# A fused backward pass on one Trainium2 core: output stores on GpSimd's queue, a last buffer of its own, and row sums scheduled earlier

## The chip, the core and the metric

The kernel runs on one core of one Trainium2 chip (trn2). A core has TensorE (PE, with its weight loads shown apart as PEld), VectorE (DVE), ScalarE (ACT), GpSimd (POOL) and SyncE (SP). All of them read their instructions in order from their own queue, and DMA transfers are issued from such a queue too. The metric is the device time of one execution in microseconds; the median of several runs is compared.

## The reference

The forward function is `x + A(xn, k, v) + B(xn)` on 2048 rows of 512 columns in bf16, and what is to be computed is its value and its gradients with respect to nine inputs.

```python
xn = _layernorm(x, axis=-1)
# A: k_shift = sum of four shifted copies of k, each times a column of shift_k
#    kv = k_shift * v
#    y  = causal convolution of kv with ssm_k along the sequence (by FFT) + kv * ssm_D
#    A  = xn * y
# B: h = (xn @ w_gate) * (xn @ w_up);  B = h @ w_down
return x + _A_ref(xn, ...) + _B_ref(xn, ...)
...
_out, _vjp = jax.vjp(_f, A_q, A_k, A_v, A_shift_k, A_ssm_k, A_ssm_D, B_w_gate, B_w_up, B_w_down)
return (_out, *_vjp(grad_out))
```

The outputs that matter here: out_0 is the value, out_1 the gradient of x, out_2 of k, out_3 of v (each 2048 x 512), out_4 of shift_k, out_5 of ssm_k, out_6 of ssm_D, out_7 and out_8 of w_gate and w_up (512 x 1376), out_9 of w_down (1376 x 512).

## The kernel before

The 2048 rows lie as 128 partitions of R = 16 rows, so a tile such as `yC` is [128, 16, 512]. The first 300 us or so (`main`, lines 858 to 876, with `side` woven into it) compute the gated network by chunks of rows, its input gradients (left in DRAM as `BX`), and the convolutions through transforms whose results are left in DRAM as `GD`. The hidden activations are left in DRAM as `HDD`.

The change is in the last stage (lines 902 to 1183). Its backbone is the generator `dw` (L1030): for each of the 11 blocks of 128 hidden columns (the last has 96) it computes the gradient of w_down (`down_grad`, L1008, matmuls L1012, cast to `od`), turns the hidden activations (`hid_t`, L832, matmuls L845, from tiles `hb` loaded from `HDD` at L791; the last three blocks come turned by a transposing DMA, `natT`, L806), and computes the gradients of w_gate and w_up (matmuls L1048 into `pu`). ACT casts `pu` into `og` (L1055), a tile with one buffer that holds two blocks, and SP stores it (L1059) after every second block and after the last one.

Four side generators are woven in by hand. `dw` yields 6 times a block, and the loop at L1176 takes one step of a side at its start index n and then every 2 or 3 yields (L1175):

- `inv_y` (L930), start 0, step 3: the inverse transform (matmuls L918 from tiles `g`, loaded at L783 two buffers deep) of y into `yC` and of the gradient `dd`, four rows at a time; DVE multiplies `dd` by v into `dks` (L948) and by the stored k-shift into `kb` (L949), which SP stores to out_3 (L950). The tiles `vb` and `kb` are loaded two buffers deep (L923, L925). Lines 953 and 954 copy three rows of `dks` across partitions. `load_kh` (L1143) loads `khC`, a copy of k with its halo rows.
- `dsk_gram` (L1065), start 27: the gradient of shift_k, matmuls L1071 from `dks` and `khC`.
- `inv_dk` (L975), start 35: the gradient of ssm_k, into `o5t`, which takes over the memory of `khC` (tag `o5k`) and is stored at L994.
- `ew` (L1162), start 10: first a load of `bb` (L1111, from `BX`), then sixteen pieces of VectorE work: `final(b)` (L1114), the value `o` and the gradient of x, `e`, for two rows of each partition, and `bwd(b)` (L1093), the gradient of k, `dk`. Each ends with a store on SP: L1124, L1139, L1105. The tiles `o0` and `e` have one buffer, `dk`, `bb`, `vb`, `kb` and `dd` have two.

Within this frame a planner of the framework orders the instructions of each engine by its own model of when they are ready; `tc.high_priority` moves DVE's products ahead, and `tc.issue_after(ins)` keeps DMA issues behind a given one on the same queue. A queue is strictly in order: an issue that waits (for the engine that makes its data, or for a buffer) holds all behind it. Except for one store of `BX` and half of the last `od`, SP issues every DMA of this stage.

Of the kernel before, what the change touches and what calls it, by code (L numbers as in the profile page):

```python
# [8 lines left out]
BF = mybir.dt.bfloat16  # L9
# [9 lines left out]
D = 512  # L19
F = 1376  # L20
R = 16
P = 128
NC4 = 4
# [167 lines left out]
def kernel(  # L191
# [24 lines left out]
    nc = tc.nc  # L216
# [409 lines left out]
    def seq(*its):  # L626
        for it in its:
            for _ in it:
                yield
# [291 lines left out]
    def load_vk(r0):  # L921
        vb = c2b.tile([P, 2, D], BF, name="vb")
        nc.sync.dma_start(vb[:], v_n[:, r0:r0 + 2, :])  # L923
        kb = c2b.tile([P, 2, D], BF, name="kb")
        DKS["kb", r0] = nc.sync.dma_start(kb[:], KS[:, r0:r0 + 2, :])  # L925
        return vb, kb
# [2 lines left out]

    def inv_y():  # L930
        gq = pend
        todo = [(sg, r0) for r0 in range(0, R, 4) for sg in (0, 1)][2:]
        for r4 in range(0, R, 4):
            gy = gq.pop(0)
            vk = [load_vk(r4), load_vk(r4 + 2)]
            for i in range(0, 4, 2):
                st1p(gy, i, yC[:, r4 + i:r4 + i + 2, :])
            if todo:
                gq.append(load_g1(*todo.pop(0)))
            yield  # L940
            gd = gq.pop(0)
            for i in range(0, 4, 2):
                r0 = r4 + i
                vb, kb = vk.pop(0)
                dd = c2b.tile([P, 2, D], BF, name="dd")
                st1p(gd, i, dd[:])
                with tc.high_priority(offset=SOON):
                    nc.vector.tensor_tensor(dks[:, r0:r0 + 2, :], dd[:], vb[:], op=ALU.mult)  # L948
                    nc.vector.tensor_tensor(kb[:], dd[:], kb[:], op=ALU.mult)  # L949
                DKS[r0] = nc.sync.dma_start(o3_n[:, r0:r0 + 2, :], kb[:])  # L950
                if r0 == 2:
                    nc.gpsimd.memset(dks[96:128, R:R + 3, :], 0.0)
                    nc.sync.dma_start(dks[0:112, R:R + 3, :], dks[1:113, 0:3, :])
                    nc.sync.dma_start(dks[112:127, R:R + 3, :], dks[113:128, 0:3, :])
            if todo:
                gq.append(load_g1(*todo.pop(0)))
            if r4 == R - 8:
                load_kh()
            yield

    def load_gk(rq):
# [13 lines left out]
    def inv_dk():  # L975
        o5t = c2.tile([P, NC4, P, R], BF, name="o5t", tag="o5k")
        o5 = out_5.rearrange("(c q) s -> c q s", q=P)
        for rq in range(4):
            gk = gks.pop(0)
            if rq == 0:  # L980
                gk_last = load_gk_last()
            for b in range(2):
                po = P2("po", [P, 2, 4, P])
                for h in range(2):
                    for i in range(4):
                        for c in range(2):
                            nc.tensor.matmul(po[:, h, i, :], lhsT=(gk_last(c, i) if rq == 3 else gk[:, c, i])[:, cs(2 * b + h)], rhs=TB.IW[:, c, :],
                                             start=(c == 0), stop=(c == 1))
                act(o5t[:, 2 * b:2 * b + 2, :, 4 * rq:4 * rq + 4], po[:].rearrange("q h r s -> q h s r"))
                if b == 1 and rq < 2:  # L990
                    gks.append(load_gk(2) if rq == 0 else None)
                if rq == 3:
                    for c in (2 * b, 2 * b + 1):
                        nc.sync.dma_start(o5[c], o5t[:, c].rearrange("q s r -> q (s r)"))  # L994
                yield
            if rq == 0:
                yield from put_dD(o5t)
# [32 lines left out]
    def dw():  # L1030
        og = None
        load_hb(2)
        for fb, (f0, fw) in enumerate(FBLK):
            last = fb + 1 == NFB
            if not last:
                down_grad(fb)
                yield
                hid_t(fb + 1, 0)
                hid_t(fb + 1, 1)
                yield  # L1040
                yield
            pu = P2("pu", [P, NC4, 2, P])
            if fb % 2 == 0:
                og = c2.tile([P, 2, NC4, 2 * P], BF, name="og")
            q0 = (fb % 2) * P
            for c in range(NC4):
                for r in range(R):
                    nc.tensor.matmul(pu[:, c, :, :fw], lhsT=xnC[:, r, cs(c)], rhs=nat_d(fb, r),  # L1048
                                     start=(r == 0), stop=(r == R - 1))
                if c == 1:  # L1050
                    yield
                    if fb + 1 in TURNED:
                        last_t(fb + 1)
                    yield
            act(og[:, :, :, q0:q0 + fw].rearrange("p t c f -> p c t f"), pu[:, :, :, :fw])  # L1055
            if fb % 2 == 1 or last:
                a = f0 - q0
                for t, o in enumerate((out_7, out_8)):
                    nc.sync.dma_start(o[:, a:f0 + fw].rearrange("(c p) f -> p c f", p=128), og[:, t, :, :q0 + fw])  # L1059
            yield  # L1060
            if last:
                down_grad(fb)
                yield
# [29 lines left out]
    def bwd(b):  # L1093
        rb = slice(2 * b, 2 * b + 2)
        dk = c2b.tile([P, 2, D], BF, name="dk")
        t = c2.tile([P, 2, D], BF, name="tk", tag="dxn")
        for j in range(4):
            src = dks[:, 2 * b + j:2 * b + j + 2, :]
            w = skb[:, j:j + 1, :].to_broadcast((P, 2, D))
            if j == 0:  # L1100
                nc.vector.tensor_tensor(dk[:], src, w, op=ALU.mult)
            else:
                nc.vector.tensor_tensor(t[:], src, w, op=ALU.mult)  # L1103
                nc.vector.tensor_tensor(dk[:], dk[:], t[:], op=ALU.add)  # L1104
        nc.sync.dma_start(o2_n[:, rb, :], dk[:])  # L1105

    FL = {}

# [5 lines left out]
    def final(b):  # L1114
        if b + 1 < 8:
            load_fin(b + 1)
        bb = FL.pop(b)
        rb = slice(2 * b, 2 * b + 2)
        tt = nc.vector.tensor_tensor
        stt = nc.vector.scalar_tensor_tensor  # L1120
        o = c2.tile([P, 2, D], BF, name="o0")
        tt(o[:], xnC[:, rb], yC[:, rb], op=ALU.mult)
        tt(o[:], o[:], bb[:, :, 0, :], op=ALU.add)
        nc.sync.dma_start(o0_n[:, rb, :], o[:])  # L1124
        e = c2.tile([P, 2, D], BF, name="e")
        tt(e[:], goC[:, rb], yC[:, rb], op=ALU.mult)
        dxn = c2.tile([P, 2, D], F32, name="dxn")
        for i in range(2):
            r = 2 * b + i
            stt(dxn[:, i], e[:, i], 1.0, bb[:, i, 1, :], op0=ALU.mult, op1=ALU.add, accum_out=s1[:, r:r + 1])  # L1130
            stt(e[:, i], dxn[:, i], 1.0, xnC[:, r, :], op0=ALU.mult, op1=ALU.mult, accum_out=s2[:, r:r + 1])  # L1131
        nc.vector.tensor_scalar(m2[:, rb], s2[:, rb], -1.0 / D, None, op0=ALU.mult)
        stt(m1[:, rb], s1[:, rb], -1.0 / D, rstd[:, rb], op0=ALU.mult, op1=ALU.mult)
        for i in range(2):
            r = 2 * b + i
            stt(dxn[:, i], xnC[:, r, :], m2[:, r:r + 1], dxn[:, i], op0=ALU.mult, op1=ALU.add)  # L1136
            nc.vector.tensor_scalar(e[:, i], dxn[:, i], rstd[:, r:r + 1], m1[:, r:r + 1], op0=ALU.mult, op1=ALU.add)
        tt(e[:], e[:], goC[:, rb], op=ALU.add)
        nc.sync.dma_start(o1_n[:, rb, :], e[:])  # L1139

    KH = []

    def load_kh():  # L1143
        khC = c2.tile([P, R + 3, D], BF, name="khC", tag="o5k")
        nc.gpsimd.memset(khC[0:1, 0:3, :], 0.0)
        with tc.issue_after(LG["g"].ins):
            nc.sync.dma_start(khC[:, 3:3 + R, :], k_n)
            nc.sync.dma_start(khC[1:113, 0:3, :], k_n[0:112, R - 3:R, :])
            nc.sync.dma_start(khC[113:128, 0:3, :], k_n[112:127, R - 3:R, :])
        KH.append(khC)  # L1150

    def every(gen, start, step):
        return [start, step, gen]
# [6 lines left out]
    tail.append(lambda: bwd(7))  # L1160

    def ew():  # L1162
        with tc.issue_after(DKS[2].ins):
            load_fin(0)
        yield
        for f in tail:
            f()
            yield

    def load_dk():  # L1170
        gks.append(load_gk(0))
        gks.append(load_gk(1))
        yield

    sides = [every(seq(inv_y(), load_dk()), 0, 3), every(dsk_gram(), 27, 2), every(inv_dk(), 35, 3), every(ew(), 10, 3)]  # L1175
    for n, _ in enumerate(dw()):  # L1176
        for sd in sides:
            if n >= sd[0]:
# [35 lines left out]
```

## Time and profile before

| | us |
|---|---|
| median of 3 runs | 489.93 (489.39 to 490.7) |
| the profiled execution | 486.87 |
| its span, first to last instruction | 485.0 |
| PE busy | 470.9 (97%) |
| DVE busy | 342.1 (71%) |
| ACT busy | 316.9 (65%) |
| POOL busy | 15.3 (3%), none of it DMA issues |
| granted TensorE clock, mean | 0.995 |
| DMA, mean over the span | 288 GB/s |

The profile is one execution. The durations quoted below come from it, so a sum is made against 486.87 and its span, not against the median. A row of the timeline reads: start, length, engine, line, operation, output <- inputs, count, and in brackets how long the engine had been idle and what ended that. "SPq" rows are DMA issues on SP's queue: their length is the time on the queue and not that of the transfer. In the list of waits a row reads: who waited for whom, total us, times, longest.

From 300 to 478 us the stage described above runs. DVE's busy share in it is uneven: 8.88 us busy of the 52.8 from 300 to 352.8, 105.94 of the 119 from 352.8 to 471.8. The DMA engines are busy for 0.94 of 319 to 351, 0.97 of 351 to 390 and 0.64 of 442 to 478.

### The profile page before, as it was taken

Reading aid. Unit: us, or ns where it says so; the run is one execution under the profiler, and the core shown is the slowest. Engines: PE = TensorE matmul, PEld = TensorE weight load, DVE = VectorE, ACT = ScalarE, POOL = GpSimd, SP = SyncE. Lnnn points to the kernel's source line nnn. Section 1 sums busy time; section 2 is a strip of 40 time slices with the busy share of each in tenths; the row PEclk is TensorE's granted clock in tenths of the full one; section 3 lists DMA queues with packets and bytes.
Section 4 is the critical chain, followed back from the end, with each engine's and each line's share of the span. In section 5 each row is a group of like instructions: output and inputs, shape, how many; then the busy total and the mean of one; then the engine's idle time right before and its main releaser. Section 6 shows DMA issues by size and latency. Waiting matters only on the chain.

```text
span 485.0 us, 10518 instructions
## 1 busy us (share of the span) xinstructions
PE 470.9 (97%) x4335; PEld 314.3 (65%) x4335; DVE 342.1 (71%) x623; ACT 316.9 (65%) x353; POOL 15.3 (3%) x31
## 2 busy tenths in 40 slices
PE   7998999999999999999999999999999999999994
PEld 7866754547647448447457744567777788777792
DVE  7889979988265667686777875013277899998880
ACT  4976896759568678779779955476567624643330
POOL 8010000000000000000000000020000000000000
PEclk9999999999999999999999999999999999999998
DMA  8999999999997968868977289998999989599717
GB/s 271 375 380 354 295 264 325 339 310 341 306 311 228 279 196 267 261 222 241 297 239 253 88 320 321 389 336 295 338 390 371 369 275 398 195 286 263 230 53 266
DMA packets 105775, 139.88 MB, mean 288 GB/s; under 512 B 33372, under 2 KB 78849, under 8 KB 104063
## 3 DMA queue, kind: packets, MB, share of 16 engines
q1 hardware_dynamic: 104142, 137.84, 85.9%
q10 hardware_dynamic: 1584, 1.36, 1.0%
q8 instruction: 34, 0.56, 0.5%
q14 instruction: 15, 0.11, 0.1%
HBM read 68.45 MB, written 63.41 MB: 272 GB/s over the span
## 4 chain that ended last, share of the span: by engine, by line
PE 57%; DVE 24%; DMA 14%; issue 2%; ACT 2%; SPq 1%; ACTq 0%; DVEq 0%
PE px L553 15%; PE pgu L510 13%; PE py L546 8%; PE pdh L516 6%; DMA out_dram<-o 5%; PE pf L368 3%; PE ps L582 3%; PE pg L611 3%; DVE tk L1103 2%; DVE dk L1104 2%; PE pu L1048 2%; DMA HDD<-hd 2%; DVE dxn L1136 2%; DVE dxn L1130 2%; DVE e L1131 2%
## 5 line engine op out<-in xcount | busy, mean ns | idle before, releaser
L553 PE MATMUL px<-WT,hd 128*128 128x512 bf16 (+1 forms) x352 | 81.1, 380 | 0.0
L1048 PEld LDWEIGHTS <-xnC 128*128 128x128 bf16 x704 | 67.1, 98 | 8.8 <-issue 0.9
L553 PEld LDWEIGHTS <-hd 128*128 128x128 bf16 (+1 forms) x352 | 32.8, 98 | 44.4 <-issue 7.7
L1048 PE MATMUL pu<-natd,xnC 128*128 128x256 bf16 x512 | 58.5, 273 | 0.2 <-ACT nath L235 0.2
L235 ACT CAST GO<-pg 128x1024 bf16<-128x1024 f32 x48 | 46.2, 1015 | 13.8 <-issue 7.2
L235 ACT CAST SP<-ps 128x1024 bf16<-128x1024 f32 x47 | 45.6, 1026 | 13.8 <-PE ps L582 11.9
L235 ACT CAST gu<-pgu 128x1024 bf16<-128x1024 f32 (+1 forms) x48 | 45.4, 945 | 13.6 <-PE pgu L510 13.5
L598 DVE TENSOR_TENSOR T<-SP 128x2048 bf16<-128x2048 bf16 x24 | 29.4, 1223 | 34.8 <-ACT SP L235 34.7
L510 PE MATMUL pgu<-xt,Wu 128*128 128x256 bf16 (+1 forms) x352 | 53.1, 274 | 0.6 <-DVE fst L238 0.4
L510 PE MATMUL pgu<-xt,Wg 128*128 128x256 bf16 (+1 forms) x352 | 52.8, 273 | 0.3 <-DMA Wg<-in_B_w_gate_dram 0.3
L516 PE MATMUL pdh<-gt,WdT 128*128 128x256 bf16 (+1 forms) x352 | 47.1, 273 | 0.1
L235 ACT CAST og<-pu 128x1024 bf16<-128x1024 f32 (+1 forms) x11 | 10.9, 993 | 50.0 <-PE pu L1048 25.6
L510 PEld LDWEIGHTS <-Wu 128*128 128x128 bf16 (+1 forms) x352 | 33.0, 100 | 14.5 <-issue 9.8
L546 PE MATMUL py<-Wd,hd 128*128 128x512 bf16 (+1 forms) x176 | 41.4, 380 | 0.0
L235 ACT CAST fst<-pf 128x1024 bf16<-128x1024 f32 x40 | 39.0, 1032 | 0.8 <-ACT dh L235 0.5
L235 ACT COPY natd<-pt 128x2048 bf16<-128x2048 bf16 x16 | 30.0, 1874 | 13.4 <-PE pt L845 13.4
L516 PEld LDWEIGHTS <-WdT 128*128 128x128 bf16 (+1 forms) x352 | 34.9, 100 | 5.2 <-issue 0.2
L510 PEld LDWEIGHTS <-Wg 128*128 128x128 bf16 (+1 forms) x352 | 34.8, 100 | 4.2 <-DMA Wg<-in_B_w_gate_dram 0.6
L530 DVE TENSOR_TENSOR hd<-gu 128x512 bf16<-128x512 bf16 (+1 forms) x48 | 19.1, 398 | 17.5 <-ACT gu L235 17.5
L531 DVE TENSOR_TENSOR hd<-gu,dh 128x1024 bf16<-128x1024 bf16 (+1 forms) x48 | 30.8, 643 | 0.8
L1012 PE MATMUL pd<-goC,nath 128*128 128x512 bf16 x128 | 30.1, 379 | 0.0
L546 PEld LDWEIGHTS <-hd 128*128 128x128 bf16 (+1 forms) x176 | 16.4, 98 | 20.5 <-issue 3.1
(176 smaller groups left out, 703.3 us busy)
## 6 DMA issues: line engine op xcount, KB each, us to landing
HDD<-hd SPq DMA_DIRECT2D x35, 384.0 KB, 3.9
FD<-fst SPq DMA_DIRECT2D x24, 512.0 KB, 4.4
X<-FD SPq DMA_DIRECT2D x24, 512.0 KB, 5.0
GD<-GO SPq DMA_DIRECT2D x24, 512.0 KB, 3.8
g<-GD SPq DMA_DIRECT2D x11, 1024.0 KB, 9.2
hb<-HDD SPq DMA_DIRECT2D x8, 1344.0 KB, 9.0
bb<-BX SPq DMA_DIRECT2D x8, 512.0 KB, 8.2
BX<-bx SPq DMA_DIRECT2D x7, 512.0 KB, 4.0
```

The source lines that it names most:

```text
L235: nc.scalar.copy(o, i)
L368: nc.tensor.matmul(pf[:, c, :], lhsT=TB.W1[:, c, :], rhs=src[:, i, :], start=True, stop=not point)
L510: nc.tensor.matmul(pgu[:w, i, t, :], lhsT=W[:, c, f0:f0 + w], rhs=xt[:, :, c, :], start=(c == 0), stop=(c == NC4 - 1))
L516: nc.tensor.matmul(pdh[:w, i, :], lhsT=WdT[:, c, f0:f0 + w], rhs=gt[:, :, c, :], start=(c == 0), stop=(c == NC4 - 1))
L530: nc.vector.tensor_tensor(hd[:fw, fb0:fb0 + n, 0, :], gu[:fw, :n, 0, :], gu[:fw, :n, 1, :], op=ALU.mult)
L531: nc.vector.tensor_tensor(hd[:fw, fb0:fb0 + n, 1:3, :], gu[:fw, :n], dh[:fw, :n].unsqueeze(2).to_broadcast((fw, n, 2, 256)), op=ALU.mult)
L546: nc.tensor.matmul(py[:], lhsT=hd[:fw, fb, 0, ss], rhs=Wd[:fw, fb, :], start=(fb == 0), stop=(fb == NFB - 1))
L553: nc.tensor.matmul(px[:], lhsT=hd[:fw, fb, t, ss], rhs=W[:fw, fb, :], start=(t == 1 and fb == 0), stop=(t == 2 and fb == NFB - 1))
L582: nc.tensor.matmul(ps[32 * q:32 * q + 32, a, :], lhsT=TB.EF[64 * a:64 * a + 64, 4 * g + q, ri].rearrange("p k j -> p (k j)"), rhs=X[64 * a ...
L598: tt(W[:].rearrange("p c a d -> p c (a d)"), A[:, i:i + 1].rearrange("p c a d -> p c (a d)").to_broadcast((P, 2, 2 * D)), B[:].rearrange(" ...
L1012: nc.tensor.matmul(pd[:fw, :], lhsT=nat_h(fb, r), rhs=goC[:, r, :], start=(r == 0), stop=(r == R - 1))
L1048: nc.tensor.matmul(pu[:, c, :, :fw], lhsT=xnC[:, r, cs(c)], rhs=nat_d(fb, r), start=(r == 0), stop=(r == R - 1))
```

## The change

It touches only the last stage:

- the stores of `o`, `e`, `dk` and `kb`, and the two copies between partitions of `dks`, are issued from GpSimd's queue instead of SP's;
- `e` gets two buffers;
- the `ew` side (the sums of `final` and `bwd`) starts at step 4 instead of 10, and its first `bb` load goes behind the latest `g` load instead of behind a `kb` store;
- the last `og` gets a tile of its own, `og1`, in a buffer of the tag `dd` (same size, [128, 2, 4, 128] bf16);
- `khC` is allocated and its first rows cleared at the start of `inv_y`; it is loaded one round later, behind the last `kb` load instead of behind the last `g` load.

```diff
     def inv_y():
         gq = pend
+        khC = c2.tile([P, R + 3, D], BF, name="khC", tag="o5k")
+        nc.gpsimd.memset(khC[0:1, 0:3, :], 0.0)
+        KH.append(khC)
...
             vk = [load_vk(r4), load_vk(r4 + 2)]
+            if r4 == R - 4:
+                load_kh()
...
-                DKS[r0] = nc.sync.dma_start(o3_n[:, r0:r0 + 2, :], kb[:])
+                nc.gpsimd.dma_start(o3_n[:, r0:r0 + 2, :], kb[:])
                 if r0 == 2:
                     nc.gpsimd.memset(dks[96:128, R:R + 3, :], 0.0)
-                    nc.sync.dma_start(dks[0:112, R:R + 3, :], dks[1:113, 0:3, :])
-                    nc.sync.dma_start(dks[112:127, R:R + 3, :], dks[113:128, 0:3, :])
+                    nc.gpsimd.dma_start(dks[0:112, R:R + 3, :], dks[1:113, 0:3, :])
+                    nc.gpsimd.dma_start(dks[112:127, R:R + 3, :], dks[113:128, 0:3, :])
             if todo:
                 gq.append(load_g1(*todo.pop(0)))
-            if r4 == R - 8:
-                load_kh()
             yield
...
             if fb % 2 == 0:
-                og = c2.tile([P, 2, NC4, 2 * P], BF, name="og")
+                og = c2b.tile([P, 2, NC4, P], BF, name="og1", tag="dd") if last else c2.tile([P, 2, NC4, 2 * P], BF, name="og")
...
-        nc.sync.dma_start(o2_n[:, rb, :], dk[:])
+        nc.gpsimd.dma_start(o2_n[:, rb, :], dk[:])
...
-        nc.sync.dma_start(o0_n[:, rb, :], o[:])
-        e = c2.tile([P, 2, D], BF, name="e")
+        nc.gpsimd.dma_start(o0_n[:, rb, :], o[:])
+        e = c2.tile([P, 2, D], BF, name="e", bufs=2)
...
-        nc.sync.dma_start(o1_n[:, rb, :], e[:])
+        nc.gpsimd.dma_start(o1_n[:, rb, :], e[:])
...
     def load_kh():
-        khC = c2.tile([P, R + 3, D], BF, name="khC", tag="o5k")
-        nc.gpsimd.memset(khC[0:1, 0:3, :], 0.0)
-        with tc.issue_after(LG["g"].ins):
+        khC = KH[0]
+        with tc.issue_after(DKS["kb", R - 2].ins):
             nc.sync.dma_start(khC[:, 3:3 + R, :], k_n)
             nc.sync.dma_start(khC[1:113, 0:3, :], k_n[0:112, R - 3:R, :])
             nc.sync.dma_start(khC[113:128, 0:3, :], k_n[112:127, R - 3:R, :])
-        KH.append(khC)
...
     def ew():
-        with tc.issue_after(DKS[2].ins):
+        with tc.issue_after(LG["g"].ins):
             load_fin(0)
...
-    sides = [every(seq(inv_y(), load_dk()), 0, 3), every(dsk_gram(), 27, 2), every(inv_dk(), 35, 3), every(ew(), 10, 3)]
+    sides = [every(seq(inv_y(), load_dk()), 0, 3), every(dsk_gram(), 27, 2), every(inv_dk(), 35, 3), every(ew(), 4, 3)]
```

## The prediction

> **What bounds the kernel now.** I read the busy time by stage first, then the timeline of the last twelve microseconds, then the waits of SP's queue, and last how long the loads take to land. The stage that the diff touches starts at about 300 us. This row of the windows view has the busy us of PE, PEld, DVE, ACT and POOL, then the granted clock, the DMA share and GB/s:
>
> ```profile
> 300.00:478.00 178.00, 177.71 (x1665) 133.04 (x1662) 114.82 (x233) 85.68 (x75) 2.74 (x2) 1.00 0.88 300
> ```
>
> PE is busy for 177.71 of 178 us at full clock. So no edit to VectorE's work, SP's queue or the stores can shorten this stretch; they can only open holes in it. DVE has 63 us of idle time. The chain of waits runs through DVE from 344 us on, which only says who released whom last. What a change can win lies after PE's last matmul. The timeline of the end:
>
> ```profile
> 474.15 0.33 PE L1048 MATMUL pu<-nat,xnC 128*128 128x192 bf16 x2
> ...
> 477.33 0.59 PE L1012 MATMUL pd<-goC,nat 128*96 128x512 bf16 x2
> ...
> 480.16 0.80 ACT L235 CAST og<-pu 128x768 bf16<-128x768 f32 x1 [9.89 <-DMA out_dram<-og]
> 480.86 0.37 ACT L235 CAST od<-pd 96x256 bf16<-96x256 f32 x1
> ...
> 481.26 0.42 DVE L238 CAST od<-pd 96x256 bf16<-96x256 f32 x1 [9.55 <-ACT od L235]
> 482.01 0.47 SPq L1025 DMA_DIRECT2D out_dram<-od  x1
> ```
>
> PE ends at 477.33 + 0.59 = 477.92. The last `og` cast could have run at 474.48, when its matmuls ended, but waited until 480.16: `og` has one buffer, and the store of its previous contents had not landed. The two casts of the last `od` stand behind it on ACT. Why that store was late shows in SP's queue:
>
> ```profile
> 467.38 4.69 SPq L1105 DMA_DIRECT2D out_dram<-dk  x2
> 472.17 0.68 SPq L1020 DMA_DIRECT2D out_dram<-od  x1
> 472.94 0.96 SPq L994 DMA_DIRECT2D out_dram<-o5t  x2
> 473.99 2.22 SPq L1059 DMA_DIRECT2D out_dram<-og  x2
> ```
>
> The previous `og` was cast by 469.35 (ACT, 468.34 + 1.01), but SP stood at the last `dk` store until DVE had made it (471.71), then issued an `od` and two `o5t` that had been ready since 461 to 462, and reached `og` at 473.99. The second half of that store landed 4.99 us after 475.08, at 480.07. So the end is a store that waited for DVE in SP's queue, and then a buffer that waited for the store.
>
> **The parts, and what each costs.**
>
> 1. *Own last buffer.* `og1` takes a slot of `dd`, whose last reader (L949) ended at 390.4. The last `og` cast then starts 0.04 us after its matmuls (the offset that ACT's `od` cast shows at 447.64 behind PE's 447.60), so at 474.52, and ends at 475.32. ACT is free when PE ends, and the first `od` cast starts at 477.92 + 0.04 = 477.96 instead of 480.86. What follows it (second cast, SP's issue 0.47, 2.0 us to landing, the end of the span at 485.0) took 4.14 us and stays. Term: 477.96 - 480.86 = **-2.90 us**. Next late is PE itself.
>
> 2. *Stores of o, e, dk, kb by GpSimd* (32 stores and the two copies of `dks`). They leave SP, whose queue from 319 to 485 waited for DVE like this (us in total, times, longest):
>
> ```profile
> SPq L1139 <- DVE e L1138: 25.5, 5, 6.5
> SPq L1105 <- DVE dk L1104: 13.6, 4, 3.9
> SPq L950 <- DVE kb L949: 10.4, 7, 4.6
> ```
>
> At the end this alone would free the `og` store: issue at 469.4, and with 4.99 us landed at about 475, so it is nearly a second remedy for the same 2.90 us and adds nothing to part 1. Elsewhere SP issues `hb`, `g`, `vb`, `bb` earlier; PE hardly waited for them, so that is worth 0.2 us at most and I take 0. On POOL the stores wait in the order in which DVE makes them, so none waits behind a later product. Behind them stands only the memset L952, whose rows bwd(7) alone needs.
>
> The cost of a store issued by POOL is in no row. Below: SP's own 0.34 us, so no loss. Above: POOL's memsets, 1.37 us each, 34 x 1.37 = 47 us of a POOL that was busy 2.74 us in the stretch. Only one of these stores is waited for by something on PE's path: `kb`, whose two buffers are refilled by SP. Call L the time from DVE's product to the landing. SP's `kb` stores landed in 2.0 to 7.0 us; with POOL's upper 1.37 that is 8.4, my value, since the memset is POOL's only row here. The upper end is the longest landing of any 256 KB store, 10.7 us, plus two issues in a row, 2.7: 13.4.
>
> What L must meet: SP puts the load of `kb` 10 ahead of the `g` load for rows 12 to 15. kb 6 is made by DVE at 346.6, `g` takes 9.5 us to land and is used by PE at 368.08, so with 0.5 for issue 346.6 + L + 10.0 <= 368.08, or L <= 11.5. The load one block earlier gives 330.0 + L + 9.7 <= 351.5, L <= 11.8. At 8.4 there is no stall; at 13.4 a stall of 1.9 us.
>
> [...]
>
> 3. *Final sums six places sooner.* In the schedule by hand, the first `bb` load moves from SP 347.01 (behind the `kb` stores) to behind the `g` load at about 327.3. With the 5.9 to 10.6 us that `bb` took to land, DVE can begin near 336 instead of 352.90. Its work from 352.8 to 471.8 is 105.94 us busy in 119, plus 2.5 us of dks/kb products that now fall inside: 336 + 108.4 = 444.4. That moves DVE's end away from the end of the kernel by 27 us; off PE's path, worth 0.
>
> 4. *e in two buffers.* SP's hold of L1126 goes; DVE only. Worth 0.
>
> 5. *khC loaded behind the last kb load* instead of behind the `g` load (364.65). kb 14 needs the buffer of kb 10, made at 363.1: 363.1 + 8.4 = 371.5, then 0.5 for issue and 13.3 to land gives 385.3. PE first reads khC at 390.09: 4.8 us spare, so 0. It turns late at L = 13.2. In exchange `hb` 5, whose load went out at 374.98 because SP stood at `e`, can go at about 366.6.
>
> **Sum.** Span 485.0 - 2.9 = 482.1; with the 1.87 us around it (486.87 - 485.0) 484.0 for the profiled execution. The median of the runs, 489.93, lies 3.06 us above that execution, and I carry the difference over: 489.93 - 2.90 = **487.0 us**. What this kernel's measurement can tell from no change is about 0.3%, 1.5 us.
>
> **Rivals.**
>
> *A: stores hold up the loads (slower).* The `kb` buffer comes free late, SP stands at the `kb` load (L925), and the `g` load behind it comes late. It decides at L = 11.5. For: in-order SP, saturated DMA (next rival), GpSimd stores of unknown length. Against: POOL has nothing else to do, and DVE is only 2.5 us busy between 335 and 352.8. Price: at L = 17, 5.5 us at `g`; khC's 3.8 us lies inside that shift. 487.0 + 5.5 = 492.5. At 13.4 it is 488.9, still counted as faster by a little.
>
> *B: the same bytes sooner, into a full DMA.* From 340 to 380 the DMA share reads 1.00 and 1.02 at 361 to 364 GB/s. Starting 17 us sooner puts about five `bb` loads, four o, four e and three dk before 380, where there were three, two, two and none: 1.0 + 0.5 + 0.5 + 0.75 = 2.75 MB more, or 7.6 us at 361 GB/s. The `g` loads have about 3.5 us spare (issue 338.9 to use 351.5, less 9.2), so up to 4 us of stall: 491.1; with the spare rate of 319 to 351 (322 GB/s) half of it: about 489. Against: `hb` and the stores had up to 20 us spare, and the peaks of the 40 slices reach 416 GB/s.
>
> *C: the end is set by something else, no change.* If the last stores queue at the DMA as before (full from 472 to 480), freeing ACT does nothing: 489.9. Against: 1 MB of `o5t` can leave at 462, and what is left after 469.4 (0.5 + 1.0 + 0.2 MB) takes 4.6 us at 370 GB/s.
>
> *D: GpSimd's descriptors hold up DVE.* DVE has 477.9 - 444.4 = 33.5 us spare over 34 stores, so it decides at 1.0 us of blocking a store. At 1.37 DVE ends at 491 and the time is about 499. Against, in the timeline: the memset on POOL at 320.44 runs beside DVE's L1122 and L1126, and these take 0.69 us as everywhere else.
>
> ```profile
> 320.44 1.37 POOL L952 MEMSET dks<- 32x1536 bf16 x1 [292.79 <-ACT yC L235]
> ...
> 320.46 0.69 DVE L1122 TENSOR_TENSOR o<-xnC,yC 128x1024 bf16<-128x1024 bf16 x1 [12.11 <-ACT yC L235]
> ...
> 321.07 0.69 DVE L1126 TENSOR_TENSOR e<-goC,yC 128x1024 bf16<-128x1024 bf16 x1
> ```
>
> **How the numbers follow.** The forecast, 487.0, holds with 0.57. A has 0.15: 0.05 short of 488.4 (faster), 0.02 within the bound, 0.08 slower. B has 0.15: 0.02 faster, 0.09 same, 0.04 slower. C has 0.08, same. D has 0.05, slower. So faster 0.64, same 0.19, slower 0.17. The low end is the forecast less the spread of the runs shown (0.65 us): 486.3; PE's end forbids more. The high end takes in B's 491.1 and leaves A's long stores and D out: 491.1.
>
> **What would show it.** Right: PE's busy share stays at 1 up to an end near 478; ACT casts `og1` within 0.1 us of its matmuls; the first `od` cast follows PE's end by 0.04 us; the span ends 4.1 us after it; DVE ends before 455; SP has no wait for L1104, L1138 or L949. Wrong: a wait of PE for `g`, `hb`, khC or `pq` between 340 and 395 (A if SP stands at L925 before it, B if the load was issued in time and landed late), a last POOL store after 480, DVE durations above 0.69 us while POOL issues (D).

## The result and the profile after

The change makes the kernel slower: 515.69 us against 490.31 for the kernel before (medians of six runs each), a ratio of 1.0515 (95% interval 1.0473 to 1.0557). The forecast was 487.0 with 491.1 as its upper end. The profiled execution took 516.29, its span is 514.6 us, 29.6 more than the 485.0 of before. Line numbers of the changed kernel are 3 to 5 higher than in the kernel before (the `dks` product is L953 there and L948 here; the `kd` product L1080 and L1077).

The windows row of the same 178 us in the changed kernel (PE, PEld, DVE, ACT, POOL busy, clock, DMA share, GB/s):

```profile
300.00:478.00 178.00, 153.69 (x1362) 110.54 (x1361) 113.28 (x233) 79.11 (x66) 21.66 (x36) 0.94 0.84 285
```

PE had 177.71 us of this window before and has 153.69 now. The list of PE's waits in the changed kernel (who waited for whom, total, times, longest) names the holes:

```profile
PE pt L845 <- DVE kd L1080: 12.2, 2, 11.0
PE pq L918 <- DMA g<-GD: 5.1, 1, 5.1
PE pk L1074 <- DMA khC<-in_A_k_dram: 4.7, 1, 4.7
...
PE pk L1074 <- DVE dks L953: 1.4, 2, 0.8
```

Before, none of these four rows exists. They sum to 23.4 us, with 0.5 more for `dskt`. PE's own work takes longer too: in the stage it is busy for 184.47 us (from 302.1 on) instead of 177.41 (from 300.3 on) with the same 1663 records, 7.1 us more, since it runs at a lower granted clock behind the long holes (0.74 from 420 to 440). And the tail, from PE's last matmul to the end of the span, went from 485.0 - 477.92 = 7.1 to 514.6 - 510.88 = 3.7 us. 23.9 + 7.1 - 3.4 = 27.6 of the 27.8 by which the stage grew. The other 1.8 of the 29.6 lie ahead of it: the same product (`bx`, L548) starts at 302.32 instead of 300.53, in code that the change does not touch.

**The tail did what was forecast.** The timeline of the changed kernel's end:

```profile
507.47 0.80 ACT L235 CAST og<-pu 128x768 bf16<-128x768 f32 x1 [4.25 <-PE pu L1051]
...
510.29 0.59 PE L1015 MATMUL pd<-goC,nat 128*96 128x512 bf16 x2
510.96 0.37 ACT L235 CAST od<-pd 96x256 bf16<-96x256 f32 x1 [2.70 <-PE pd L1015]
...
511.81 0.34 SPq L1028 DMA_DIRECT2D out_dram<-od  x1
```

The last `og` cast waits for its own matmuls and no longer for a store; the first `od` cast follows PE by 0.08 us (510.96 against 510.88). So the 3.4 us are won, at the end of a PE that is 33 us late.

**The holes come through VectorE.** First, how it worked before, between two rounds of `inv_y` (timeline of DVE, kernel before):

```profile
344.09 0.69 DVE L948 TENSOR_TENSOR dks<-dd,vb 128x1024 bf16<-128x1024 bf16 x1 [12.91 <-ACT dd L235]
344.70 0.69 DVE L949 TENSOR_TENSOR kb<-dd,kb 128x1024 bf16<-128x1024 bf16 x1
...
352.90 0.69 DVE L1123 TENSOR_TENSOR o<-o,bb 128x1024 bf16<-128x1024 bf16 x1 [6.32 <-DMA bb<-BX]
...
360.66 0.69 DVE L948 TENSOR_TENSOR dks<-dd,vb 128x1024 bf16<-128x1024 bf16 x1 [1.32 <-ACT dd L235]
```

DVE waits for `dd`, makes the `dks` and `kb` products, and only then stands for something of the sums (`bb`). Now the same two rounds in the changed kernel:

```profile
346.79 0.69 DVE L1141 TENSOR_TENSOR e<-e,goC 128x1024 bf16<-128x1024 bf16 x1
354.36 0.69 DVE L1129 TENSOR_TENSOR e<-goC,yC 128x1024 bf16<-128x1024 bf16 x1 [6.88 <-ACT od L235]
354.96 0.69 DVE L953 TENSOR_TENSOR dks<-dd,vb 128x1024 bf16<-128x1024 bf16 x1
355.56 0.69 DVE L954 TENSOR_TENSOR kb<-dd,kb 128x1024 bf16<-128x1024 bf16 x1
...
371.66 0.69 DVE L1129 TENSOR_TENSOR e<-goC,yC 128x1024 bf16<-128x1024 bf16 x1 [4.13 <-DMA out_dram<-e]
...
378.31 0.68 DVE L953 TENSOR_TENSOR dks<-dd,vb 128x1024 bf16<-128x1024 bf16 x1
```

At 347.5 DVE comes to an `e` product (L1129) whose buffer is free only when the store of an older `e` has landed. That store was issued by POOL at 347.77; the two `e` stores of this stretch took 6.5 and 7.1 us to land, and 347.77 + 6.5 = 354.27, just ahead of 354.36. (The bracket names ACT's cast of `od`, which ended at 354.28, at the same moment. But the product reads `goC` and `yC`, and the rows of `yC` that it reads were cast by 339.88; in the next round, and at such an `e` in run 7 below, the bracket names the store.) The `dks` product stands right behind it in DVE's queue and starts at 354.96, 10.9 us later than before (1.8 of it from the first 300 us), and in the next round at 378.31 instead of 360.66.

SP then does what rival A said, for a reason that A did not have: it stands at the loads of `vb` and `kb`, whose buffers those products release (waits of SP's queue in the changed kernel, from 319 us on):

```profile
SPq L923 <- DVE dks L953: 21.9, 3, 11.8
SPq L925 <- DMA out_dram<-kb: 16.0, 4, 8.0
```

Behind them the `g` load of the last rows goes out at 365.08 instead of 354.71, and `khC` at 387.25 instead of 364.65. These are PE's holes of 5.1 us (up to 375.31) and 4.7 us (up to 404.82).

The third and largest hole, 11.0 us up to 428.13, is DVE's order once more. The first group of `pk` matmuls was done at 409.41 + 0.41 = 409.82; the `kd` product that frees its PSUM came at 427.22:

```profile
401.94 0.69 DVE L1125 TENSOR_TENSOR o<-xnC,yC 128x1024 bf16<-128x1024 bf16 x1 [7.00 <-DMA out_dram<-o]
...
413.50 0.69 DVE L1129 TENSOR_TENSOR e<-goC,yC 128x1024 bf16<-128x1024 bf16 x1 [2.94 <-DMA out_dram<-e]
...
427.22 0.85 DVE L1080 TENSOR_TENSOR kd<-pk,ident 64x256 f32<-64x256 f32 x2
```

Between 394.95 and 427.22 DVE stands for 10.5 us at stores of the sums (7.00, 0.58, 2.94) and otherwise works through sums that the planner has written ahead of `kd`. Before, it ran at 394.95:

```profile
394.95 0.85 DVE L1077 TENSOR_TENSOR kd<-pk,ident 64x256 f32<-64x256 f32 x2
```

The order itself can be read off the two programs. DVE's instructions from the first `o` product on, with the sums shortened (`o`, `e` the first products, `o+` the sum with `bb`, `s` the row sums, `E!` the last step of `e`, `dk` the pieces of `bwd`, KD the `kd` product), kernel before and changed kernel:

```
before:  o e DKS kb DKS kb dk dk DKS kb DKS kb o+ s E! DKS kb DKS kb o o+ e s E! dk dk dk o o+ e s DKS kb DKS kb E! dk dk dk KD ...
changed: o e e DKS kb DKS kb dk dk o+ s o E! e DKS kb DKS kb o+ s o E! o+ dk dk e o dk s DKS kb DKS kb o+ E! dk dk o dk e o+ dk s o dk E! DKS kb DKS kb ... KD ...
```

Before, an `o` and an `e` into a buffer just handed to a store stand behind the `dks` and `kb` pairs (`E! DKS kb DKS kb o o+ e`). In the changed kernel they stand ahead of them (`o E! e DKS kb DKS kb`). Nobody wrote this; the planner did.

### The profile page after: what moved, and what is told of

The parts are those of the page before. It is cut to its first block, busy times and chain, and to the rows that moved or that the text cites. A ratio compares the mean times of both kernels' runs of the same rounds, so it can differ in the third digit from the quotient of the medians.

```text
span 514.6 us, 10536 instructions
## 1 busy us (share of the span) xinstructions
PE 479.4 (93%) x4335; PEld 318.3 (62%) x4335; DVE 340.8 (66%) x623; ACT 317.4 (62%) x353; POOL 34.3 (7%) x65
## 4 chain that ended last, share of the span: by engine, by line
PE 62%; issue 15%; DMA 14%; DVE 4%; POOL 2%; ACT 2%; SPq 0%; ACTq 0%; POOLq 0%; DVEq 0%
PE px L553 14%; PE pgu L510 13%; PE py L546 7%; PE pdh L516 6%; PE pu L1051 6%; PE pf L368 4%; PE pd L1015 3%; DMA out_dram<-e 3%; PE ps L582 3%; PE pg L611 3%; DMA go_b<-in_grad_out_dram 2%; DMA HDD<-hd 2%; DMA bb<-BX 2%; DMA Wg<-in_B_w_gate_dram 2%; DMA out_dram<-o 1%
## 5 line engine op out<-in xcount | busy, mean ns | idle before, releaser
L553 PEld LDWEIGHTS <-hd 128*128 128x128 bf16 (+1 forms) x352 | 32.8, 98 | 44.4 <-issue 7.7
L235 ACT CAST og<-pu 128x1024 bf16<-128x1024 f32 (+1 forms) x11 | 10.9, 993 | 49.4 <-PE pu L1051 49.4
L845 PE MATMUL pt<-ident,hb 128*128 128x128 bf16 x336 | 24.1, 228 | 12.4 <-DVE kd L1080 12.2
L845 PEld LDWEIGHTS <-hb 128*128 128x128 bf16 x336 | 21.7, 103 | 17.8 <-DVE kd L1080 13.5
```

The source lines that it names most:

```text
L235: nc.scalar.copy(o, i)
L553: nc.tensor.matmul(px[:], lhsT=hd[:fw, fb, t, ss], rhs=W[:fw, fb, :], start=(t == 1 and fb == 0), stop=(t == 2 and fb == NFB - 1))
L845: nc.tensor.transpose(pt[:, r, :fw], hs[:, (r % 2) * 128:(r % 2) * 128 + 128], ident[:fw, :fw])
```

## Experiments

Two theories stood at first. **G**: issuing stores on GpSimd costs by itself. **S**: the earlier start of the sums does. The runs below ended S and left little of G, and a third, **P**, took their place: moving a store to another queue changes the order that the planner writes for VectorE, and the order costs. In what follows "before" is the kernel before in the same batch: 489.2 us for the first four runs, 489.77 for the next four, 490.07 for the last three.

### 1. The changed kernel with the sums back at their start

```diff
-    ... every(ew(), 4, 3)]
+    ... every(ew(), 10, 3)]
```

> The changed kernel with the sums at place 10 again, everything else of the change kept. Theory S (the sooner sums are the cause: on VectorE's in-order queue they stand, waiting, ahead of the dks products): the loss of 25 us goes, about 487. Theory G (the stores by GpSimd are the cause: an o or e store takes 6.5 to 10 us to land, and VectorE waits for its buffer ahead of the dks products, wherever the sums start, since e 2 still stands before the dks products of the third round): still above 500.

Measured: 512.56 us, ratio 1.0482 (1.0433 to 1.0532). PE waits for `kd` 11.3 us, for `dskt` 4.4, for `dks` 3.4, for `khC` 2.3. The early start is not the cause; S falls.

### 2. The changed kernel with all its stores on SP

```diff
-                nc.gpsimd.dma_start(o3_n[:, r0:r0 + 2, :], kb[:])
+                nc.sync.dma_start(o3_n[:, r0:r0 + 2, :], kb[:])
...
-        nc.gpsimd.dma_start(o1_n[:, rb, :], e[:])
+        nc.sync.dma_start(o1_n[:, rb, :], e[:])
```

(and so for the copies of `dks`, `dk` and `o`)

> The changed kernel with all these stores on SP again, the rest of the change kept. Theory S: still slow, above 505, since the sums start at 4. Theory G: the loss goes, 487 to 490.

Measured: 490.04 us, ratio 1.0015 (0.9988 to 1.0043); span 486.0. PE waits for `g` once, 2.9 us, and for `khC` once, 0.9.

25 us hang on which queue issues the stores. What is left is small change: the tail is 3.5 us here too (PE ends at 482.48), and 3.8 us of waits for loads give it back. Runs 1 and 2 both came out as G had said; what separates G from P are runs 5, 6 and 10.

### 3. The kernel before with only the sums sooner

```diff
-        with tc.issue_after(DKS[2].ins):
+        with tc.issue_after(LG["g"].ins):
             load_fin(0)
...
-    ... every(ew(), 10, 3)]
+    ... every(ew(), 4, 3)]
```

> The kernel before with the sums at place 4 alone (first bb load behind the latest g load). Theory S: slower than 500. Theory G: within 1.5 us of 490, as TensorE sets the end and SP's stores land in 2 to 6 us.

Measured: 491.4 us, ratio 1.005 (1.0022 to 1.0078).

```profile
PE pq L918 <- DMA g<-GD: 4.7, 1, 4.7
```

The prediction's "worth 0" for part 3 was wrong even with every store left on SP. The price is that of rival B (up to 4 us of stall, 491.1 us), but that is luck, since B's mechanism is not there: its sign was a load "issued in time" that "landed late". Here SP stood at the `e` store until DVE had made `e`, and issued the `g` load behind it late:

```profile
354.41 1.08 SPq L1059 DMA_DIRECT2D out_dram<-og  x2
360.45 0.34 SPq L1139 DMA_DIRECT2D out_dram<-e  x1
...
364.54 0.53 SPq L783 DMA_DIRECT2D g<-GD  x1
```

In the kernel before the same load went out at 354.71 and landed in 9.5 us; here it landed in 9.7. The tail is 3.4 us (PE ends at 486.77, the span at 490.2) though `og` has one buffer in this run: the first sign that the tail does not hang on the buffer.

### 4. The kernel before with only the last buffer of its own

```diff
-                og = c2.tile([P, 2, NC4, 2 * P], BF, name="og")
+                og = c2b.tile([P, 2, NC4, P], BF, name="og1", tag="dd") if last else c2.tile([P, 2, NC4, 2 * P], BF, name="og")
```

> The kernel before with the last og in a buffer of its own and nothing else. Both theories, and the prediction's tail term: 2.9 us off, 487.4 beside 490.3 for the kernel before; the last og cast 0.04 us behind its matmuls.

Measured: 489.42 us, ratio 0.9996 (0.9963 to 1.0029). The last `og` cast runs at 475.62, right behind its matmuls, as forecast; PE ends at 479.03, ACT's `od` cast follows at 479.11; and the span still ends at 487.2. SP's queue, this run:

```profile
469.29 4.69 SPq L1105 DMA_DIRECT2D out_dram<-dk  x2
474.08 1.78 SPq L1020 DMA_DIRECT2D out_dram<-od  x1
475.95 0.88 SPq L994 DMA_DIRECT2D out_dram<-o5t  x2
476.92 2.07 SPq L1059 DMA_DIRECT2D out_dram<-og  x2
479.09 1.68 SPq L994 DMA_DIRECT2D out_dram<-o5t  x2
480.86 2.57 SPq L1059 DMA_DIRECT2D out_dram<-og  x2
483.53 0.77 SPq L1025 DMA_DIRECT2D out_dram<-od  x1
```

SP stands at the `dk` stores as before, and the six rows behind it, ten issues, take 9.75 us together (1.78 + 0.88 + 2.07 + 1.68 + 2.57 + 0.77). The last `od`, made by DVE at 479.9, is issued at 483.53. So the last buffer alone moves the wait from ACT to SP, the 2.9 us that the expectation had are not there, and the outcome is that of rival C (no change). C's full DMA is there too, with a share of 0.98, 1.06 and 0.99 in 478 to 480, 480 to 482 and 482 to 484.3, so this run alone does not tell the queue from the DMA. Runs 8 and 9 do.

### 5. and 6. Each kernel's order on the other one's queues

Both kernels were built with VectorE's 200 instructions of the last stage held in a given order, by edges between neighbours that add no wait:

```python
by = {i.name: i for i in nc.cur_bb.bb.instructions}
for p, q in zip(ORDER, ORDER[1:]):
    tc.add_manual_dep(by[f"I-{q}"], f"I-{p}", mybir.DependencyInfo(mybir.DependencyClass.NoSync, ...), ...)
```

Run 5 is the changed kernel (stores on GpSimd) with the order of the kernel of run 2; run 6 is the kernel of run 2 (stores on SP, no store on GpSimd at all) with the order of the changed kernel.

> The changed kernel, its stores on GpSimd, with VectorE's instructions of the last stage chained in the order that the planner wrote when the same stores were on SP (the run with all stores on SP again). Theory P (the move of the stores harms only through the planner: on a queue of their own it takes them to land sooner than they do, and writes the next o and e products, which wait for those landings, ahead of the dks and kd products): 487 to 492. Theory G (the stores by GpSimd harm by themselves, through their landing, their descriptors or the DMA): stays above 505.

> The reverse: the stores on SP, and VectorE's instructions in the order that was planned for the changed kernel. Theory P: as slow as the changed kernel or slower, above 505, without one store by GpSimd. Theory G: 487 to 491, as with the stores on SP and their own order.

Run 5: 494.41 us, ratio 1.0093 (1.0061 to 1.0126). Run 6: 522.75 us, ratio 1.0692 (1.0648 to 1.0737). PE's waits in run 5:

```profile
PE pk L1074 <- DMA khC<-in_A_k_dram: 5.4, 1, 5.4
```

PE's and then DVE's in run 6:

```profile
PE pu L1051 <- DVE kd L1080: 14.2, 1, 14.2
PE pq L918 <- DMA g<-GD: 3.4, 1, 3.4
```

```profile
DVE o L1125 <- DMA out_dram<-o: 35.2, 5, 14.1
```

The order makes the kernel slow with not one store on GpSimd, and the other order takes 21 of the 25 us out with all of them there. (In run 6 SP stands at the stores as well, 20.4 us for `dk` and 16.7 for `e`, so its 33 us are not the price of the order alone.) So P holds for most of the loss, and G falls as its cause. But run 5 missed P's 487 to 492: some 4 us over run 2 stay. They go with `khC`, which is issued at 386.06 instead of 381.62, behind loads of `kb` that wait for stores (SP's queue in run 5):

```profile
SPq L925 <- DMA out_dram<-kb: 15.3, 5, 7.9
```

These stores landed in a median of 6.7 us from GpSimd, and of 5.0 from SP in run 2. That is rival A's path at a small price, and a rest of G that these runs do not rule out.

### 7. and 8. The move alone, and the two stores that matter

Run 7 is the kernel before with all those stores and the two copies on GpSimd, the first `bb` load behind the `g` load, and nothing else. Run 8 is the kernel before with the last buffer of run 4 and with the last two `dk` stores alone on GpSimd:

```diff
-        nc.sync.dma_start(o2_n[:, rb, :], dk[:])
+        (nc.gpsimd if b > 5 else nc.sync).dma_start(o2_n[:, rb, :], dk[:])
```

> The kernel before with the move of the stores to GpSimd alone (the first bb load behind the latest g load): sums at 10, one e buffer, old og, khC as before. Theory P: its planned order has an e and an o product ahead of the dks products of the third round and the kd products deep in the sums, so slow, 500 to 512. Theory G: also slow, 505 or more. If it is at 490, the move needs e's second buffer or khC's place as well.

> The kernel before with the last og in its own buffer and only the last two dk stores on GpSimd. VectorE's planned order is that of the kernel before, and SP no longer stands at the last dk store. Theory P and the tail term of the prediction: 2.5 to 3.5 us off, about 486 beside 489.2. Theory G: two stores can hardly harm, about the same.

Run 7: 512.31 us, ratio 1.0467 (1.0427 to 1.0508), where G had it and at the top of P's 500 to 512. Its PE waits:

```profile
PE pk L1071 <- DVE dks L948: 14.2, 2, 13.2
PE pt L845 <- DVE kd L1077: 7.2, 3, 3.1
```

The move is enough by itself: DVE's order differs from that of the kernel before, in the same way as above (`o+ s o E! e DKS kb DKS kb` after the second round), and nothing that the planner was given differs but the queue of the stores and copies and the place of one load. That it takes a store on a queue of its own to be over sooner than it is would explain this; its model was not looked into, so that is argued and not shown.

Run 8: 485.5 us, ratio 0.9918 (0.9887 to 0.995), faster than both kernels, with an interval that leaves 1 out. DVE's order is that of the kernel before, PE ends at 478.78, and the span at 482.4, where the forecast's sum had 482.1. With SP free from 464 on, the same stores go out as they are made, and the DMA engines are busy for only 0.39 of 476 to 480: the full DMA of run 4 came of SP's late issues.

### 9. The two stores without the buffer

The edit of run 8 to the `dk` store, and no other.

> The kernel before, with only the last two stores of dk issued by GpSimd; og keeps its one buffer and every other engine keeps its order. Theory Q (the tail is set by SP's queue, in which the last dk stores stand for 4.69 us ahead of finished o5t, od and og): with SP free, the og store of the blocks before goes out at about 470.3, lands about 475, and the last og cast runs by 475.5 even with one buffer, so PE's end sets the end as in the run with the buffer as well: span 482 to 483, time 485 to 486.5, ratio 0.990 to 0.995. Theory B1 (the prediction's: the single buffer of og is what holds ACT's od cast): the cast still waits for the landing of the og store to about 478.5 or later, and the span stays above 484: ratio 0.996 to 1.000.

Measured: 485.1 us, ratio 0.9921 (0.9888 to 0.9955); span 483.2. SP's queue, and then ACT, in this run:

```profile
471.10 1.01 SPq L1059 DMA_DIRECT2D out_dram<-og  x2
...
480.54 0.34 SPq L1025 DMA_DIRECT2D out_dram<-od  x1
```

```profile
476.28 0.80 ACT L235 CAST og<-pu 128x768 bf16<-128x768 f32 x1 [4.29 <-PE pu L1048]
```

With one buffer of `og` the last cast waits for its matmuls and for no store, since SP issued the store ahead of it as soon as it was made (471.10). So the whole gain at the end is that of SP's queue, and runs 8 and 9 do not differ by more than their intervals.

### 10. and 11. How much of it the order is, and an order by hand

Run 10 is run 7 with the last buffer and with DVE's instructions held in the order of the kernel before. Run 11 is the changed kernel with the sums of each pair of rows issued behind the latest `kb` product:

```diff
+    def final_behind(b):
+        with tc.issue_after(DKS["mul"].ins):
+            final(b)
...
-        tail.append(lambda b=b: final(b))
+        tail.append(lambda b=b: final_behind(b))
```

> The kernel before, with all stores of o, e, dk and kb and the two copies of dks issued by GpSimd and the last og in a tile of its own, and with VectorE's instructions of the last stage held, by ordering edges that cost no wait, in the order that the planner gave the kernel before. The same move of the stores without the held order measured 512.3 us. Theory P (the loss is the order that the planner writes for VectorE once the stores stand in GpSimd's queue): no hole above 2 us before kd or dks, SP free at the end, span 482 to 485, time 485 to 488, ratio 0.990 to 0.997. Theory G (GpSimd's queue or its descriptors cost by themselves): 500 us or more.

> The changed kernel, with the sums of each pair of rows issued behind the latest kb product on VectorE, which puts every pair dks and kb ahead of the o and e products of the rows before; the four groups kd still come behind sums that wait. Theory P (VectorE's order): the holes at g, dks and khC go, the hole at kd stays (up to the 12 us of the changed kernel, or more, since three of the sums' pieces now stand right before the first kd): 495 to 506, ratio 1.01 to 1.033. Theory G (GpSimd's queue itself): no gain, 512 to 516.

Run 10: 493.25 us, ratio 1.0073 (1.0045 to 1.0102), so 19 of run 7's 23 us are gone, but not all, and the forecast of 485 to 488 was missed. Its PE waits:

```profile
PE ptd L1003 <- DVE dskt L238: 3.9, 1, 3.9
PE pt L845 <- DVE kd L1077: 1.6, 2, 1.1
```

DVE stands for 6.5 us at stores of `e` (3.87 of it at 430, for the one buffer) and for 12.6 at `bb`; its copy of `dskt`, the longest wait of PE, comes at 440.00 instead of 433.99. With the same order of DVE as in the kernel before, the stores of `e` and `kb` land later (medians 5.8 and 6.6 us, 3.9 and 5.2 before). An order made for other arrivals is not free; which arrival costs the 8 us over run 8, and how much of it is the queue itself, was not tried further and stays open.

Run 11: 512.74 us, ratio 1.0486 (1.0433 to 1.0538), above P's 495 to 506 and inside G's 512 to 516. But the holes went where the edit put the order right and stayed where it did not:

```profile
PE pt L845 <- DVE kd L1080: 15.2, 3, 12.3
PE pq L918 <- DMA g<-GD: 2.8, 2, 2.0
```

The waits for `dks` and `khC` are gone, that for `g` is halved, and `kd`, whose place the edit leaves to the planner, costs 17.4 us in all (15.2, and 2.2 at L990). By time alone this run does not tell P from G; its waits do.

## Why the prediction was wrong, point by point

**What bounds the kernel: right.** PE had no gap from 300 to 478, so the stretch could only get worse, and what could be won lay in the tail. The changed kernel shows both: 3.4 us won in the tail, 31.0 lost in the stage.

**Part 1, the last buffer, -2.90: the size was near, the cause wrong.** The spans of runs 8 and 9 are 2.6 and 1.8 us shorter than before, their medians 4.3 and 5.0 (intervals 2.4 to 5.5 and 2.2 to 5.5). That the size fits is in part luck, since the buffer did not bring it. The step "the store of its previous contents had not landed ... a buffer that waited for the store" was true of the trace and still not the lever. The buffer alone gave 0.9996 (run 4); freeing SP of two `dk` stores gave 0.992 with it and without it (runs 8 and 9). The prediction saw that part 2 would be "nearly a second remedy for the same 2.90 us"; it was the only one. What was missed: `og1`'s own store and the last `od` still had to leave by the same queue, behind the same 4.69 us, and then met a full DMA. What follows the first `od` cast, the 4.14 us that "stays", took 3.5 in run 8 (478.87 to 482.4).

**Part 2, the stores on GpSimd, 0: the step that failed.** L, over which the prediction argued, was not what failed. In the changed kernel an issue took 0.54 us of POOL (29 of 34), between the two bounds, and the landings are like those on SP (minimum, median, maximum us):

| store | before, SP | run 2, SP | changed, GpSimd |
|---|---|---|---|
| o | 2.4 / 4.7 / 10.7 | 5.2 / 8.6 / 11.6 | 2.4 / 4.2 / 9.9 |
| e | 2.6 / 3.9 / 5.2 | 2.0 / 5.1 / 9.7 | 2.3 / 5.2 / 7.1 |
| kb | 2.0 / 5.2 / 7.0 | 4.5 / 5.0 / 7.7 | 4.1 / 5.7 / 8.5 |

The sentence that failed is "kb 6 is made by DVE at 346.6": both decisions, 346.6 + L and 363.1 + L, took the times of DVE's products from the trace of before, as if its order were given. They were 10.9 and 17.7 us late, 1.8 of that from the first 300 us. The rest, 9.1 and 15.9, takes the limits of 11.5 and 13.2 for L down to 2.4 and to less than nothing, where the fastest `kb` store took 4.1. So the stall came whatever L was.

**Part 3, the sums sooner, "off PE's path, worth 0": wrong twice.** By itself it costs 4.7 us at `g` (run 3), since SP stands at a store that DVE makes late. In the changed kernel the sums are on PE's path, since they stand in one in-order queue with `dks`, `kb` and `kd`, and `o` and `e` wait for stores. DVE did begin early (the first sum with `bb` at 338.46, forecast "near 336"), yet it ended at 474.2, not at 444.4, having stood in the queue and not for want of time. The prediction's "DVE has 63 us of idle time" and "DVE is only 2.5 us busy between 335 and 352.8" counted busy time where position decides: at 347.5 to 354.4 DVE is idle and the `dks` product cannot pass.

**Part 4, two buffers of e, 0.** It did not keep DVE from waiting for `e` (7.1 and 6.9 us in the changed kernel). Alone it was not tried.

**Part 5, khC, 0.** 4.8 us spare were given; `kb` 10 was made so late that the load of `kb` 14, and `khC` behind it, had to wait, and `khC` went out at 387.25, 2.8 us ahead of the forecast's first use, and cost 4.7 us. The dependence on "kb 10, made at 363.1" was the same failed step.

**The rivals.** A's picture came (SP at L925, `g` late), not its condition: the `kb` product that ended at 357.46 was stored, and the next load into its buffer was out by 364.98 (SP, 364.44 + 0.54), so L was at most 7.5, under 11.5. B's price came in run 3, by another mechanism: the load was issued late and landed as fast as before. C was right for part 1 alone, in the outcome and in the full DMA; but the DMA was full because SP had issued late. D is ruled out: DVE's products take 0.68 to 0.69 us beside POOL's issues as elsewhere. The case that happened was not among them. The prediction asked of each wait what it would be if a duration changed, and never what the planner would do with the move, although the description of the kernel says that it orders each engine by its own model.

**POOL's issues beside DVE's work.** Two of them in the changed kernel:

```profile
364.57 0.54 POOL L1142 DMA_DIRECT2D out_dram<-e  x1 [5.68 <-DVE e L1141]
...
381.09 0.74 POOL L955 DMA_DIRECT2D out_dram<-kb  x1 [0.67 <-DVE kb L954]
```

The second lies for 0.62 us beside DVE's L1140 (1.00 us from 380.71; L1137 in the kernel before), and is 0.20 us longer. It is one row, and not clear of what an issue varies by anyhow: the first issue of the stage took 0.81 beside `dks` and `kb` products alone. Nothing waited for the 0.20 us.

## What to carry to other kernels

Where a planner orders an engine, a DMA moved to another queue is also a change to that engine's order: compare the engine's instructions of both programs before you price anything by the old trace's times. An in-order engine with idle time (DVE of the changed kernel, idle from 347.5 to 354.36) can still be the bound, when an instruction that waits for a buffer stands ahead of one that another engine needs; read what stands behind each wait, not the busy share. And when a buffer waits for a store, look first at why the store was issued late: here two stores moved off SP's queue (0.992) did what the buffer could not (0.9996) and what moving all of them turned into a loss (1.05). Last, a stall of the size that a rival gave is not yet that rival: look whether the load was issued late or landed late.

## What the runs showed of the hardware

PE ran slow behind the long holes. Two 20 us windows of the changed kernel, without a hole and around the longest one (same columns as above; the clock is third from the end, 0.98 and 0.74):

```profile
380.00:400.00 20.00, 20.00 (x190) 15.71 (x188) 11.81 (x25) 12.56 (x9) 3.33 (x6) 0.98 0.93 335
...
420.00:440.00 20.00, 11.74 (x119) 9.21 (x120) 19.73 (x41) 6.08 (x4) 2.69 (x5) 0.74 0.64 229
```

In run 11 the same 14 transposes show it beside each other:

```profile
417.80 1.68 PE L845 MATMUL pt<-ident,hb 128*128 128x128 bf16 x14 [12.32 <-DVE kd L1080]
423.76 0.95 PE L845 MATMUL pt<-ident,hb 128*128 128x128 bf16 x14 [0.85 <-DVE kd L1080]
```

1.68 us behind a hole of 12.32, 0.95 behind one of 0.85. So a hole cost more than its length here: 23.9 us of holes came with 7.1 us of slower matmuls in the stage.

0.95 / 1.68 is 0.57. In the changed kernel the granted clock was 0.50 from 375.3 to 380.7, from 404.8 to 408.0 and from 428.1 to 431.9, behind the holes of 5.1, 4.7 and 11.0 us, and 0.99 to 1.00 from 302 to 375, 381 to 404, 409 to 417 and 433 to 470. The eight L918 matmuls took 3.60 us behind the first of these holes and 1.89 at 320.31. PE was busy for 5.39, 2.77 and 3.77 us of the three stretches, 11.93 together. Estimated from these numbers, with half of that time owed to the halved clock, they cost 6.0 us; measured were 7.1, and where the rest lies was not tried.

An issue on SP's queue took longer while a backlog was worked off: the last six rows of SP (`od`, `o5t`, `og`, `o5t`, `og`, `od`) take 9.75 us in run 4, where they are issued in one go, and 5.05 in run 8 (0.38 + 0.90 + 0.93 + 1.18 + 1.32 + 0.34), where each goes out when its data are made. The DMA engines were full in the first case (0.98 to 1.06 from 478 on) and busy for 0.68 of 464 to 480.1 in the second; whether the backlog or the full DMA stretches the issues was not tried.
